# Weight conversion with one VectorE instruction for the low word, two buffers, six weight buffers, and left-over loads by another queue

## The chip, the cores and the metric

The kernel runs on one core of one Trainium2 chip. The metric is the device time of one execution in microseconds (us). One core has five engines with instruction streams of their own: TensorE (matrix products; PE in the profile, its weight loads PEld), VectorE (DVE), ScalarE (ACT), GpSimd (POOL) and SyncE (SP, which here only issues DMA transfers). Each engine works through its stream in the order of the program; semaphores hold an instruction until what it needs is there. ScalarE and GpSimd can issue transfers too.

## The reference

Attention of pooled queries, then a block with a two-dimensional Fourier transform, a normalization and a feed-forward part; cut to what matters:

```python
def _attn_ref(q, k, v):                       # q, k, v: (4, 8, 1152, 64) float32
    q_pool = q.reshape(B, H, S // 2, 2, D).mean(axis=3)
    scores = np.matmul(q_pool, k.transpose(0, 1, 3, 2)) / np.sqrt(D)
    attn = np.exp(scores - scores.max(axis=-1, keepdims=True))
    attn = attn / (attn.sum(axis=-1, keepdims=True) + 1e-9)
    return np.matmul(attn, v)                 # (4, 8, 576, 64)

def _moe_ref(x, w_ch1, w_ch2):                # x: (4, 576, 512); w_ch1 512x2048, w_ch2 2048x512
    u = x + np.real(fft(fft(x, axis=1), axis=2)).astype(np.float32)
    un = (u - mean(u)) / np.sqrt(var(u) + 1e-6)         # over the last axis
    return u + np.maximum(un @ w_ch1, 0.0) @ w_ch2
```

The two weights arrive as float64. There is no such type on the engines, so the kernel takes each number apart by its two 32-bit words.

## The kernel before

**Attention.** There are 32 heads (4 batches of 8), taken two at a time: 16 pairs of 5 units each. For a unit, TensorE makes scores in pieces of 384 columns from a high and a low part of the queries (line 220), VectorE scales each piece into the tile "sp" and keeps a running minimum (line 222), ScalarE takes the exponential (line 234), TensorE transposes the result in groups of four (line 247), ScalarE and sometimes VectorE copy each group out (line 250), and TensorE multiplies with the values (line 263). Ahead of a head, prep_head() has GpSimd add the two halves of each query (line 186) and take the low part of the keys (line 189); the high part of the queries is a cast on ScalarE (line 194), and GpSimd makes the low part "ql" from it (line 197). The loads of a head are issued in lines 126 and 127, the ones for queries, keys and values by SyncE, one by GpSimd.

**After a batch's last head** its middle part runs (dft() and norm(): Fourier products, then a normalization of which lines 550 to 602 concern us), and then its feed-forward part ffn(): 32 blocks in four groups, each group four blocks of the first weight (F1, f1()) and four of the second (F2, f2()). A block is 12 matmuls of 512 columns (lines 689 to 691: three products of high and low parts, four times); after an F1 block ScalarE takes the ReLU (line 708) and VectorE the remainder (line 709). Middle and feed-forward parts of one batch are laid between the attention units of the next by a planner: every step of these generators gives a time in ns, "credit" holds what may still be laid in, and a heap of due times ("after") holds what comes later. The planner's times set the order in which instructions are written, and so the order on each engine. Batches 0 to 2 work on 512 of the 576 columns of a batch; the 64 left over of each are stored to the DRAM tensor "left" (line 608), and the last batch takes these 192 columns as part of its own two blocks of 384 (loaded in lines 593 and 758).

**Conversion.** convert() makes one of the 32 weight blocks usable. It loads 512 KB of words into "wraw" (three buffers), and then: ScalarE the absolute value of the high word ("wa"), VectorE a clamp (631) and a shift and mask (633), ScalarE a scaled copy of the low word into "rest" (635), VectorE the float32 nearest by its bits into "wb" (639) and its power of two back into "wa" (642), ScalarE the high part (646), and GpSimd three passes in two halves each (649): rest times the power of two, the remainder of the high part, their sum. The result goes back to HBM (655) and is loaded again for each use, four times in all, by wload() (681) into one of the three buffers of the pool "w", two blocks ahead. "wa", "rest" and "wb" share the four buffers of the tag "cv". The list "inside" lets one conversion at a time be between its first ScalarE instruction and GpSimd's passes; up to three are under way in all, and a new one begins at the earliest 8 to 10 us of planned time after the last. They are taken in the order in which the feed-forward part wants them: four of W1, four of W2, and so on. I number them 0 to 31.

**The drain.** The tile pool "x" for attention's results has five buffers, so before the attention may go on past a certain point of batch 1, drain() lets the feed-forward part of batch 0 finish, with what conversions are left. Block n of batch 0 waits in the planner until block n + 2's weight is converted.

## Time and profile before

| | us |
|---|---|
| median of 3 runs (lowest to highest) | 1023.06 (1022.12 to 1026.41) |
| time of the profiled execution | 1021.06 |
| its span, first to last instruction | 1019.3 |
| TensorE busy | 968.8 (95%) |
| VectorE busy | 602.5 (59%) |
| ScalarE busy | 529.1 (52%) |
| GpSimd busy | 396.0 (39%) |

The mean granted clock of TensorE is 0.990 of full speed. In forty slices of the span TensorE is at nine tenths or more in most; the other engines are loaded in the first half, where attention and conversions run, and hardly at all in the last eighth, where only the last feed-forward part is left. How to read it: TensorE's busy time is the sum to beat, and what a change elsewhere can win or lose is in TensorE's idle stretches, about 50 us in all, and in stretches at a lower granted clock. A busy share of another engine says little by itself.

### The profile page before, as it was taken

To read this page: it belongs to the slowest core of one execution; us is meant where nothing else is said; L and a number is where in the kernel's file an instruction comes from. 1 tells how busy PE (TensorE), PEld (TensorE's weight loads), DVE (VectorE), ACT (ScalarE), POOL (GpSimd) and SP (SyncE) were. 2 spreads that over 40 slices of the span, in tenths; PEclk is the share of its full clock that TensorE was granted. 3 is DMA by queue.
4 is the path that set the end of the run, shared out by engine and by line. 5 is a ranking of instruction groups with operands and counts; after the bars stand their busy time and mean duration, and the time that the engine had idled before them with its cause. 6 is when DMAs were issued, how large, how long until landed. Compare 5 with 4: busy or idle time off the path is not lost.

```text
span 1019.3 us, 19742 instructions
## 1 busy us (share of the span) xinstructions
PE 968.8 (95%) x7392; PEld 841.5 (83%) x7392; DVE 602.5 (59%) x1526; ACT 529.1 (52%) x1033; POOL 396.0 (39%) x577
## 2 busy tenths in 40 slices
PE   6999988999999999978999999999999999899998
PEld 5898877777788887867888888788888878799998
DVE  5557787888756798866544465745644274422222
ACT  5777877758755575565644454535744221301100
POOL 3555678766666786874523232222400000000000
PEclk9999999999899999999999999999999999999999
DMA  6645458645385877566565453345432445733434
GB/s 181 176 142 183 130 189 255 191 139 167 119 255 208 280 242 235 182 235 197 175 194 164 135 184 120 90 150 161 130 116 83 145 137 165 219 131 128 128 124 124
DMA packets 62515, 170.91 MB, mean 168 GB/s; under 512 B 16770, under 2 KB 20242, under 8 KB 62420
## 3 DMA queue, kind: packets, MB, share of 16 engines
q1 hardware_dynamic: 58100, 151.96, 47.4%
q0 software_dynamic: 4320, 17.70, 5.5%
q8 instruction: 58, 0.95, 0.4%
q14 instruction: 37, 0.30, 0.1%
HBM read 146.88 MB, written 22.75 MB: 166 GB/s over the span
## 4 chain that ended last, share of the span: by engine, by line
PE 51%; DVE 3%; DMA 2%; ACT 1%; issue 1%; POOL 1%; SPq 0%; DVEq 0%; ACTq 0%
PE f L689 7%; PE f L691 6%; PE f L690 6%; PE o L263 6%; PE s L220 6%; PE t L247 5%; PE t L689 5%; PE t L691 5%; PE t L690 5%; DMA w<-w 1%; DVE sp L222 1%; DMA qr<-in_q 1%; PE f L509 1%; PE t L509 1%; ACT pt L250 0%
## 5 line engine op out<-in xcount | busy, mean ns | idle before, releaser
L222 DVE TENSOR_SCALAR_CACHE_REDUCE sp<-s,bia 128x384 f32<-128x384 f32 x288 | 177.5, 616 | 89.6 <-PE s L220 67.5
L220 PE MATMUL s<-ks,qh 128*128 128x384 f32 x480 | 185.1, 386 | 17.3 <-ACT qh L164 6.3
L234 ACT ACTIVATE sp<-sp,bia 128x1152 f32<-128x1152 f32 x144 | 180.2, 1255 | 5.7 <-DVE sp L222 5.4
L250 ACT COPY pt<-t 128x512 f32<-128x512 f32 (+2 forms) x243 | 124.7, 527 | 98.7 <-PE t L247 95.5
L263 PE MATMUL o<-pt,vs 128*64 128x128 f32 (+1 forms) x2880 | 168.1, 271 | 1.1 <-DVE pt L250 0.9
L263 PEld LDWEIGHTS o<-pt,vs 128*64 128x64 f32 x2880 | 148.9, 140 | 23.4 <-issue 20.1
L220 PE MATMUL s<-ks,ql 128*128 128x384 f32 x480 | 164.1, 342 | 0.9 <-POOL ql L197 0.9
L247 PE MATMUL t<-ident,sp 128*128 128x128 f32 x1045 | 151.7, 277 | 3.0 <-DVE sp L222 2.0
L247 PEld LDWEIGHTS t<-ident,sp 128*128 128x128 f32 x1045 | 121.0, 141 | 25.5 <-issue 7.0
L189 POOL TENSOR_TENSOR ks<-kr,ks 64x288 fp32r<-64x288 f32 x120 | 101.9, 880 | 37.3 <-issue 15.9
L220 PEld LDWEIGHTS s<-ks,qh 128*128 128x128 f32 x480 | 92.2, 192 | 28.1 <-ACT pt L250 10.1
L220 PEld LDWEIGHTS s<-ks,ql 128*128 128x128 f32 x480 | 92.6, 193 | 2.1 <-POOL ql L197 1.2
L709 DVE SCALAR_TENSOR_TENSOR g<-f,g 128x512 fp32r<-128x512 f32 (+1 forms) x49 | 32.5, 663 | 99.4 <-ACT g L708 99.4
L708 ACT ACTIVATE g<-f 128x512 fp32r<-128x512 f32 (+1 forms) x49 | 28.2, 576 | 120.0 <-PE f L691 120.0
L222 DVE TENSOR_SCALAR_CACHE_REDUCE sp<-s 128x384 f32<-128x384 f32 x144 | 78.7, 547 | 9.6 <-PE s L220 8.3
L197 POOL TENSOR_TENSOR ql<-qr,qh 128x288 fp32r<-128x288 f32 (+2 forms) x75 | 54.2, 747 | 75.6 <-ACT qh L194 74.6
L689 PE MATMUL f<-unh,w 128*128 128x512 f32 (+1 forms) x196 | 77.4, 395 | 6.3 <-DMA w<-w 5.8
L649 POOL TENSOR_TENSOR rest<-rest,wa 128x256 f32<-128x256 f32 x64 | 48.8, 781 | 88.9 <-DVE wa L642 69.9
L186 POOL TENSOR_TENSOR qr<-qr 128x288 f32<-128x288 f32 x60 | 48.1, 820 | 78.5 <-DMA qr<-in_q 78.5
L689 PE MATMUL f<-g,w 128*128 128x512 f32 (+1 forms) x192 | 76.0, 396 | 2.3 <-DMA w<-w 1.1
L691 PE MATMUL f<-unl,w 128*128 128x512 f32 (+1 forms) x196 | 75.1, 383 | 0.0
L690 PE MATMUL f<-unh,w 128*128 128x512 f32 (+1 forms) x196 | 74.8, 381 | 0.0
(146 smaller groups left out, 1749.8 us busy)
## 6 DMA issues: line engine op xcount, KB each, us to landing
w<-w SPq DMA_DIRECT2D x128, 512.0 KB, 3.6
qr<-in_q SPq DMA_DIRECT2D x30, 576.0 KB, 4.3
ks<-in_k POOLq DMA_DIRECT2D x30, 576.0 KB, 6.2
wraw<-in_w SPq DMA_DIRECT2D x32, 512.0 KB, 3.9
w<-wraw SPq DMA_DIRECT2D x32, 512.0 KB, 3.0
vs<-in_v SPq DMA_DIRECT2D x32, 288.0 KB, 7.0
kr<-in_k SPq DMA_DIRECT2D x30, 288.0 KB, 5.4
out<-x SPq DMA_DIRECT2D x12, 256.0 KB
```

The lines of the kernel that those rows point to most:

```text
L189: nc.gpsimd.tensor_tensor(ks[D:, c], kr[D:, c], ks[D:, c].bitcast(F32), op=ALU.subtract)
L197: nc.gpsimd.tensor_tensor(ql[:, z], qr[:, 0, x:y], qh[:, z].bitcast(F32), op=ALU.subtract)
L220: nc.tensor.matmul(ps, lhsT=l, rhs=k, start=i == 0, stop=i == len(ops) - 1)
L222: nc.vector.tensor_scalar(sp[n, j][:, c], ps, -0.0625, bt[:, pc - 1:pc] if pc else None, op0=ALU.mult, op1=ALU.min, accum_out=bt[:, pc:pc ...
L234: last_exp[0] = nc.scalar.activation(t, t, AF.Exp, bias=bia.pop((n, j))[:, 2:3], scale=-1.0, accum_out=den[pr][:, col:col + 1]).ins
L247: nc.tensor.transpose(ps[:, i * P:i * P + P], sp[k][:, c * P:(c + 1) * P], ident)
L250: (nc.vector.tensor_copy if eng == "v" else nc.scalar.copy)(pt[:, :o], ps[:, :o])
L263: nc.tensor.matmul(po[y * D:y * D + D, :w], lhsT=qkv[2 * pr + y][3][:, c, :], rhs=pt[:, o:o + w], start=c == 0, stop=c == NKC - 1)
L649: nc.gpsimd.tensor_tensor(o[:, c], x[:, c], y[:, c], op=op)
L689: nc.tensor.matmul(ps, lhsT=ah, rhs=bh, start=first, stop=False)
L690: nc.tensor.matmul(ps, lhsT=al, rhs=bh, start=False, stop=False)
L691: nc.tensor.matmul(ps, lhsT=ah, rhs=bl, start=False, stop=last)
```

## The change

Four things change. In convert(), the scaled copy on ScalarE and GpSimd's first pass go; VectorE makes low word times 2^-52 times the power of two in one instruction (line 640 of the new file), written over "wa". So a conversion has two tiles of the tag "cv" instead of three, and GpSimd two passes instead of three. The planner's times in it change: five steps of 700 (or 1000) ns where there were four, 2000 instead of 3000 and 2600 instead of 3000 behind GpSimd's work. When no conversion is left, wload() takes three of six weight tiles from the three "wraw" buffers, so that six are there in all, and ffn() loads up to four blocks ahead. And the loads of the left-over columns in norm() go out by ScalarE's queue instead of SyncE's.

```diff
-                        nc.sync.dma_start(y[i][:, :, HT:].bitcast(F32), left[x, :, 2 * i:2 * i + 2, t * 96:t * 96 + 96])
+                        nc.scalar.dma_start(y[i][:, :, HT:].bitcast(F32), left[x, :, 2 * i:2 * i + 2, t * 96:t * 96 + 96])
@@ convert()
-        yield 6500 if going else 7000
+        yield 7000 if going else 7000
         while inside:
             yield 400
         inside.append(f)
         high, low = w[:, :, 1], w[:, :, 0]
-        a = cvp.tile([P, 512], F32, tag="cv", name="wa", bufs=4)
-        ai = a.bitcast(I32)
+        a, t = (cvp.tile([P, 512], F32, tag="cv", name=x, bufs=4) for x in ("wa", "wb"))
+        ai, ti = a.bitcast(I32), t.bitcast(I32)
+        step = 700 if going else 1000
 
         nc.scalar.activation(a, high.bitcast(F32), AF.Abs)
         yield 900 if going else 1400
         nc.vector.tensor_scalar(a, a, WORD_MIN, WORD_MAX, op0=ALU.max, op1=ALU.min)
-        yield 700 if going else 1000
+        yield step
         nc.vector.tensor_scalar(ai, ai, 3, 0x3FFFFFF8, op0=ALU.logical_shift_left, op1=ALU.bitwise_and)
-        rest = cvp.tile([P, 512], F32, tag="cv", name="rest", bufs=4)
-        nc.scalar.activation(rest, low.bitcast(U32), AF.Copy, scale=2.0 ** -52)
-        yield 700 if going else 1000
-        t = cvp.tile([P, 512], F32, tag="cv", name="wb", bufs=4)
-        b = t.bitcast(I32)
-        nc.vector.scalar_tensor_tensor(b, high, -0x40000000, ai, op0=ALU.bitwise_and, op1=ALU.bitwise_or)
-
-        yield 700 if going else 1000
-        nc.vector.tensor_scalar(ai, b, -0x800000, None, op0=ALU.bitwise_and)
-        yield 700 if going else 1000
+        yield step
+        nc.vector.scalar_tensor_tensor(ti, high, -0x40000000, ai, op0=ALU.bitwise_and, op1=ALU.bitwise_or)
+        yield step
+        nc.vector.tensor_scalar(ai, ti, -0x800000, None, op0=ALU.bitwise_and)
+        yield step
+        nc.vector.scalar_tensor_tensor(a, low.bitcast(U32), 2.0 ** -52, a, op0=ALU.mult, op1=ALU.mult)
+        yield step
         h = w.rearrange("p c x -> p (c x)").rearrange("p (x c) -> p x c", x=2)
         hi, lo = h[:, 0, :], h[:, 1, :]
         nc.scalar.copy(hi.bitcast(F32R), t)
-        for o, x, y, op in ((rest, rest, a, ALU.mult), (t, t, hi.bitcast(F32), ALU.subtract), (lo.bitcast(F32R), t, rest, ALU.add)):
+        for o, x, y, op in ((t, t, hi.bitcast(F32), ALU.subtract), (lo.bitcast(F32R), t, a, ALU.add)):
             for c in (slice(0, 256), slice(256, 512)):
                 nc.gpsimd.tensor_tensor(o[:, c], x[:, c], y[:, c], op=op)
         if not going:
-            yield 3000
+            yield 2000
         inside.pop()
-        yield 3000 if going else 1500
+        yield 2600 if going else 1500
@@ wload()
-        w = wp.tile([P, 2, 512], F32R, tag="w", name=nm)
+        src = (wp, "w", 3)
+        if not todo and not busy:
+            turns[0] += 1
+            if turns[0] % 6 < 3:
+                src = (cvp, "wraw", 3)
+        w = src[0].tile([P, 2, 512], F32R, tag=src[1], name=nm, bufs=src[2])
@@ ffn()
-            load(n + 2)
+            for x in (2,) if todo or busy else (2, 3, 4):
+                load(n + x)
```

The changed planner times move conversions against the rest of the program. GpSimd's stream around conversion 4 (lines 649 before and 647 after; first row the end of conversion 3) and the preparation of the next head of queries (memsets of "qh" and "ql", the sum of q's halves "qr", the low parts "ks" and "ql"), before:

```order
L649 TENSOR_TENSOR wraw<-wb,rest 128x256 x2
L126 DMA ks<-in_k 128x1152
L649 TENSOR_TENSOR rest<-rest,wa 128x256 x2
L649 TENSOR_TENSOR wb<-wb,wraw 128x256 x2
L649 TENSOR_TENSOR wraw<-wb,rest 128x256 x2
L137 MEMSET qh 128x64
L138 MEMSET ql 128x64
L186 TENSOR_TENSOR qr<-qr 128x288 x2
L189 TENSOR_TENSOR ks<-kr,ks 64x288 x4
L197 TENSOR_TENSOR ql<-qr,qh 128x288 x2
```

And after:

```order
L647 TENSOR_TENSOR wraw<-wb,wa 128x256 x2
L126 DMA ks<-in_k 128x1152
L137 MEMSET qh 128x64
L138 MEMSET ql 128x64
L186 TENSOR_TENSOR qr<-qr 128x288 x2
L189 TENSOR_TENSOR ks<-kr,ks 64x288 x4
L197 TENSOR_TENSOR ql<-qr,qh 128x288 x2
L647 TENSOR_TENSOR wb<-wb,wraw 128x256 x2
L647 TENSOR_TENSOR wraw<-wb,wa 128x256 x2
```

The conversion that stood ahead of the head's preparation stands behind all of it.

GpSimd's stream at the last head ahead of the drain, whose "ql" rows are the last of line 197 before the drain; the numbers tell tiles apart. Before:

```order
L649 TENSOR_TENSOR wb_5636<-wb_5636,wraw_5428 128x256 x2
L649 TENSOR_TENSOR wraw_5428<-wb_5636,rest_5617 128x256 x2
L137 MEMSET qh_5734 128x64
L138 MEMSET ql_5735 128x64
L186 TENSOR_TENSOR qr_5571<-qr_5571 128x288 x2
L189 TENSOR_TENSOR ks_5570<-kr_5572,ks_5570 64x288 x4
L197 TENSOR_TENSOR ql_5735<-qr_5571,qh_5734 128x288
L197 TENSOR_TENSOR ql_5735<-qr_5571,qh_5734 128x224
L197 TENSOR_TENSOR ql_5735<-qr_5571,qh_5734 128x64
L649 TENSOR_TENSOR rest_5726<-rest_5726,wa_5675 128x256 x2
L649 TENSOR_TENSOR wb_5758<-wb_5758,wraw_5588 128x256 x2
```

And after:

```order
L186 TENSOR_TENSOR qr_5432<-qr_5432 128x288 x2
L189 TENSOR_TENSOR ks_5431<-kr_5433,ks_5431 64x288 x4
L647 TENSOR_TENSOR wb_5475<-wb_5475,wraw_5342 128x256 x2
L647 TENSOR_TENSOR wraw_5342<-wb_5475,wa_5474 128x256 x2
L197 TENSOR_TENSOR ql_5587<-qr_5432,qh_5586 128x288
L197 TENSOR_TENSOR ql_5587<-qr_5432,qh_5586 128x224
L197 TENSOR_TENSOR ql_5587<-qr_5432,qh_5586 128x64
L647 TENSOR_TENSOR wb_5616<-wb_5616,wraw_5511 128x256 x2
L647 TENSOR_TENSOR wraw_5511<-wb_5616,wa_5615 128x256 x2
L647 TENSOR_TENSOR wb_5685<-wb_5685,wraw_5636 128x256 x2
```

Before, conversion 26 is the last ahead of the head's preparation and 27 is the first behind "ql"; after, the one between "ks" and "ql" is 24, and 25 and 26 follow. So 27 conversions stood ahead of that "ql", and 25 stand there now. TensorE has eight feed-forward blocks of batch 0 in the drain before, nine after; up to about 375 us of the trace its stream is the same in both.

SyncE's stream at the start of batch 3 (weights "w", results "out", the left-over columns "unh" and "unl"), before:

```order
L681 DMA w_10208<-w_15_6019 128x1024
L723 DMA out<-x 128x512
L593 DMA unh_10227<-left 128x2x96
L593 DMA unh_10228<-left 128x2x96
L593 DMA unl_10229<-left 128x2x96
L593 DMA unl_10230<-left 128x2x96
L593 DMA unh_10243<-left 128x2x96
L593 DMA unh_10244<-left 128x2x96
L593 DMA unl_10245<-left 128x2x96
L593 DMA unl_10246<-left 128x2x96
L681 DMA w_10257<-w_0_1465 128x1024
L723 DMA out<-x 128x512
```

And after:

```order
L684 DMA w_10073<-w_15_5923 128x1024
L684 DMA w_10099<-w_0_1463 128x1024
L727 DMA out<-x 128x512
L684 DMA w_10148<-w_1_1689 128x1024
L727 DMA out<-x 128x512
L684 DMA w_10165<-w_2_1903 128x1024
```

The eight transfers from "left" are gone from here, and the first weight of batch 3 (source w_0) directly follows the last of batch 2. On ScalarE they stand in two groups of four, each ahead of two of the four casts of line 599 that batch 3 needs (before, the casts follow line 571 at once):

```order
L571 ACTIVATE dg<-ident,vt 96x96 x6
L593 DMA unh_10118<-left 128x2x96
L593 DMA unh_10119<-left 128x2x96
L593 DMA unl_10120<-left 128x2x96
L593 DMA unl_10121<-left 128x2x96
L599 CAST unh_10118<-d 128x2x288
L599 CAST unh_10119<-d 128x2x288
L593 DMA unh_10134<-left 128x2x96
L593 DMA unh_10135<-left 128x2x96
L593 DMA unl_10136<-left 128x2x96
L593 DMA unl_10137<-left 128x2x96
L599 CAST unh_10134<-d 128x2x288
```

The order on TensorE has three feed-forward blocks of batch 2 behind line 581's two matmuls and ahead of batch 3's first block, where two stood before.

## Rows read from the trace of the kernel before

**Rows 1.** Stretches: bounds, length, busy PE, PEld, DVE, ACT, POOL; clock, DMA share, GB/s.

```profile
87.00:275.00 188.00, 171.68 (x1581) 145.27 (x1579) 150.31 (x388) 142.12 (x282) 131.27 (x187) 0.96 0.56 175
...
430.00:478.00 48.00, 38.70 (x225) 31.39 (x225) 31.57 (x57) 27.21 (x48) 33.67 (x47) 0.93 0.67 226
```

**Rows 2.** TensorE's waits, 87 to 275 us: total us, times, longest us.

```profile
PE f L247 <- ACT pt L250: 3.7, 5, 1.6
PE s L220 <- ACT pt L250: 3.2, 5, 1.1
PE s L220 <- DVE sp L222: 2.3, 4, 0.8
...
PE t L247 <- DVE sp L222: 1.2, 2, 0.7
```

**Rows 3.** TensorE's waits for weight loads: whole run, then 430 to 478 us.

```profile
PE f L689 <- DMA w<-w: 6.8, 3, 3.1
...
PE f L689 <- DMA w<-w: 4.1, 2, 3.1
```

**Rows 4.** Groups by line, 87 to 275 us: busy us, mean ns, idle ahead.

```profile
L635 ACT ACTIVATE rest<-wraw 128x512 f32<-128x512 uint32 x13 | 9.0, 689 | 0.0
...
L649 POOL TENSOR_TENSOR rest<-rest,wa 128x256 f32<-128x256 f32 x25 | 18.5, 756 | 41.7 <-DVE wa L642 38.4 <-ACT wraw L646 3.3
...
L639 DVE SCALAR_TENSOR_TENSOR wb<-wraw,wa 128x512 int32<-128x512 int32 x13 | 12.5, 963 | 0.1
```

**Rows 5.** Three lines of the conversion, whole run: ns least/middle/most, first to last us.

```profile
L639 DVE SCALAR_TENSOR_TENSOR wb<-wraw,wa x32: 670/690/3799, 93.6 to 470.6; 128x512 int32<-128x512 int32 x32
...
L642 DVE TENSOR_SCALAR wa<-wb x32: 408/422/1047, 95.3 to 471.3; 128x512 int32<-128x512 int32 x32
...
L646 ACT CAST wraw<-wb x32: 605/622/627, 95.6 to 471.3; 128x512 fp32r<-128x512 f32 x32
```

**Rows 6.** Timeline near 158 us: start us, length us, engine; idle time ahead in brackets.

```profile
157.12 0.67 ACT L194 CAST qh<-qr 128x576 fp32r<-128x576 f32 x1 [3.37 <-POOL qr L186]
...
158.33 0.45 PE L220 MATMUL s<-ks,qh 128*128 128x384 f32 x1 [1.14 <-ACT pt L250]
...
159.93 3.85 PE L263 MATMUL o<-pt,vs 128*64 128x128 f32 x36
```

**Rows 7.** Stretch 160 to 163.5 us, columns as in rows 1.

```profile
160.00:163.50 3.50, 3.50 (x35) 3.50 (x36) 1.62 (x6) 3.13 (x6) 3.00 (x4) 0.51 0.58 98
```

**Rows 8.** Timeline of the drain; SPq is SyncE's queue of transfers.

```profile
445.57 1.59 POOL L649 TENSOR_TENSOR wraw<-wb,rest 128x256 fp32r<-128x256 f32 x2
...
447.19 0.32 SPq L655 DMA_DIRECT2D w<-wraw  x1
...
450.86 0.43 SPq L620 DMA_DIRECT2D wraw<-in_w  x1
...
454.22 0.77 PE L689 MATMUL f<-unh,w 128*128 128x512 f32 x1 [3.09 <-DMA w<-w]
...
467.71 0.39 PE L689 MATMUL f<-g,w 128*128 128x512 f32 x1
...
470.55 2.19 PE L263 MATMUL o<-pt,vs 128*64 128x128 f32 x36
...
477.41 0.33 SPq L655 DMA_DIRECT2D w<-wraw  x1
```

**Rows 9.** Timeline behind the drain: a load of queries, and a wait.

```profile
483.06 0.42 SPq L126 DMA_DIRECT2D qr<-in_q  x1
...
493.51 0.45 PE L220 MATMUL s<-ks,qh 128*128 128x384 f32 x1 [1.77 <-ACT pt L250]
```

**Rows 10.** Timeline at the start of batch 3.

```profile
873.34 0.98 SPq L593 DMA_DIRECT2D unh<-left  x2
...
877.70 0.41 SPq L681 DMA_DIRECT2D w<-w  x1
...
881.38 0.41 PE L689 MATMUL f<-unh,w 128*128 128x384 f32 x1 [2.69 <-DMA w<-w]
```

1 line of the change is left out of this document (added).

## The prediction, made before the result was known

> **What bounds the kernel now.** I read the stretches first. TensorE works nearly all the time, so a change pays only where TensorE waits or runs on its lower clock level. It waits in three places that this change touches. Between 87 and 275 us it is busy 171.7 of 188 us at a mean granted clock of 0.96, with VectorE at 150.3 us (80%), ScalarE at 142.1 and GpSimd at 131.3 [rows 1]: here attention, the first Fourier stage and weight conversions share three engines. Between 430 and 478 us it is busy 38.7 of 48 us at clock 0.93 [rows 1]: the drain of batch 0, where feed-forward blocks follow each other and each needs a weight that has only just been converted. And it stands once near 880 us, at the start of batch 3. In between it has hardly any gaps.
>
> The waits say who ends them. From 87 to 275 us the four largest entries are 3.7 and 3.2 us ended by ScalarE's copies of transposes and 2.3 and 1.2 us ended by VectorE's score pieces [rows 2]. Waits of TensorE for a weight load come to 6.8 us in the whole run, three of them, and two with 4.1 us are in the drain [rows 3]; the third, 6.8 - 4.1 = 2.7 us, is the one near 880 us.
>
> **One conversion.** Removed: ScalarE's scaled copy of the low word, 13 in the stretch 87 to 275 for 9.0 us, and GpSimd's product in two halves, 18.5 us there [rows 4]. Added: one VectorE instruction with two inputs from SBUF, of the shape and kind of line 639. That line takes 0.67 us at the least, 0.69 in the middle, 3.80 at worst [rows 5], and 0.963 on average in this stretch [rows 4]. I take 0.69: 13 x 0.69 = 9.0 us more on VectorE, 150.3 + 9.0 = 159.3 of 188 us (85%). So VectorE does not become the bound on average, but it works in program order, and a score piece behind the new instruction comes 0.69 us later. Which part lands on the path? Of the 10.4 us in the four entries, VectorE ended 3.5 (34%) [rows 2]; 0.34 x 9.0 = 3.1 us. The bounds are 0 (hidden in VectorE's idle 20%) and 9.0 (all on the path).
>
> Against it stands the relief. At 157 us ScalarE sat 3.37 us on the cast of q, because GpSimd added q's halves only after a conversion; the transposes' copies stood behind that cast, TensorE waited 1.14 us for one of them, and soon after, its next 36 matmuls took 3.85 us [rows 6]. From 160 to 163.5 us the granted clock was 0.51, which is the lower of the engine's two levels, 1.2 GHz [rows 7]; a group of the same shape at the higher one takes 2.19 [rows 8]. In the new order GpSimd has that conversion behind q's halves, not before them. I count the 1.14 and the 3.85 - 2.19 = 1.7, that is 2.8 us. Of the other ScalarE-ended waits, 6.9 - 1.1 = 5.8 us, I take a third, 1.9, since GpSimd loses one of three equal parts of each conversion. Together 4.7; the bounds are 0 (a new wait forms elsewhere) and 8.6 (all of them go). Net of this stretch: 3.1 - 4.7 = **-1.6 us**.
>
> The Trainium skill, page "SBUF — State Buffer", section "Who interferes with whom", says that a VectorE instruction with two SBUF inputs contends with a GpSimd instruction that reads SBUF, and the second to issue blocks until the first is done. Line 639's middle value of 0.69 us, next to its least, shows that most are not blocked [rows 5]. By the page alone every overlap would cost up to one GpSimd operation; the second rival below prices that from rows.
>
> **Two buffers, and where the conversions stand.** Before, three tiles of the four-deep tag "cv" go into a conversion, so its third tile waits for GpSimd's last addition of the conversion before; now two go in, and conversion n needs only n-2 finished. That allows overlap. But the planner's steps changed too: a conversion holds "inside" for five steps instead of four. The order shows the effect: before the drain GpSimd has 27 conversions (0 to 26) ahead of the last remainder of q; now 25. Two more conversions therefore fall into the drain, and one more feed-forward block (nine instead of eight).
>
> The drain's price, by rows. Before: GpSimd ends conversion 27 at 445.57 + 1.59 = 447.16 us, SyncE writes it out at 447.19, and TensorE starts on it, loaded back, at 454.22 after a wait of 3.09 [rows 8]: 7.1 us from GpSimd's end to TensorE. Four writes later it is 477.41, so 7.6 us apiece. The last block, on weight 29, ends where the next attention group starts, 470.55 [rows 8].
>
> After: conversion 25 stands where 27 stood. Its own GpSimd part is 1.5 us shorter, and I give it 1 us more because one block fewer is ahead: written at 447.2 - 2.5 = 444.7. What sets the pace from there? Three raw buffers, and VectorE works off a block's remainder between two steps of a later conversion, so three conversions form a ring: write to TensorE 7.0, block 470.55 - 467.71 = 2.8 [rows 8], ReLU and remainder 1.3 (two passes of that size, 0.62 + 0.69), mask 0.42, new product 0.69, high part 0.62 [rows 5], GpSimd 4 x 0.76 = 3.0 [rows 4]: 15.8 us, or 5.3 per conversion. Weight 29 is written at 444.7 + 4 x 5.3 = 465.9, TensorE starts on it at 473.0 and ends at 475.8, against 470.55: **+5.3 us**. Bounds: if SyncE's pair is the limit (447.19 to 450.86 + 0.43 is 4.1 us [rows 8]) the end is 444.7 + 16.4 + 7.1 + 2.8 = 471.0, +0.5. At the pace of before, 7.6, it is 485.0, +14.4. The lower clock level in the longer waits is inside that upper bound. I take 5.3: the wait of one conversion for the one before, which the pace of 7.6 holds, is gone, and the ring is what is left.
>
> After the drain a wait goes: at 493.51 TensorE waits 1.77 us on a chain that begins at q's load, issued at 483.06 behind a weight's write [rows 9]. With attention about 5 us later and that load not later, the wait is covered: **-1.8** (0 if the load slips as well).
>
> **Left-over columns by ScalarE's queue, six weight buffers.** SyncE issues eight transfers from "left" ahead of batch 3's first weight, 0.98 us for two of them; the weight goes out at 877.70 and TensorE waits 2.69 us until 881.38 [rows 10]. Four pairs at 0.98 are 3.9 us, so without them the weight lands before it is wanted: **-2.7**. On ScalarE's queue they cost the same 3.9 us, two groups of 1.9, each ahead of two casts that batch 3's first block needs, and the VectorE remainders wait for those. The cover is TensorE's: the order has three feed-forward blocks (3 x 2.8 = 8.4 us) behind line 581's matmuls and ahead of batch 3's first block, where two stood. Two groups of issue and four casts fit. If they do not, up to 1.9 us comes back. Loads four blocks ahead instead of two gain nothing else: only three weight waits exist [rows 3], and two lie in the drain, where the new depth is not yet on. Their price is none that I see: the "wraw" tiles that lend room hold no conversion any more by then.
>
> **Sum.** -1.6 + 5.3 - 1.8 - 2.7 = -0.8 us. The profiled execution took 1021.06 us (span 1019.3), 2.0 under the median 1023.06; on the median's base **1022.3 us**. About 0.5% (5.1 us) is what a measurement of this kernel can tell from no change.
>
> **Rivals.** First, the drain costs nothing: conversions overlap so well in their two buffers that SyncE's 4.1 us is the pace (+0.5), and the early relief is full (8.6 against 3.1): -5.5 + 0.5 - 1.8 - 2.7 = -9.5, **1013.6 us**. For it: the conversions' engines are at 57 to 70% in the drain [rows 1], and the wait for the predecessor is the one that two buffers remove. Against it: VectorE's and ScalarE's program order ties each conversion to a block two or three back.
>
> Second, slower: VectorE is blocked beside GpSimd from 87 to 275 us. The new instruction then costs 0.963 us like line 639 there [rows 4], 12.5 us in all, and as ScalarE's score work waits on VectorE, half of it lands on the path without any relief: +6.3 + 5.3 - 1.8 - 2.7 = +7.1, **1030.2 us**. It decides against the kernel once over 4.3 of the 12.5 us land there (4.3 + 5.3 - 4.5 = 5.1). This is what the rule of the Trainium skill told above would give if it held at every overlap. Against it: the middle one of the 32 instructions of line 639 takes 0.69, near their least of 0.67 [rows 5], and GpSimd has a third less to do.
>
> Third, the drain keeps its pace of 7.6: -1.6 + 14.4 - 4.5 = +8.3, **1031.4 us**. For it: two more conversions stand there. Against it: two buffers.
>
> Fourth, the last part does not do what it says: ScalarE's queue delays batch 3's casts as long as SyncE delayed the weight. Then the 2.7 stays: **1025.0 us**.
>
> **How the numbers follow.** Forecast 0.36; first rival 0.33, its milder forms (1013 to 1018) with it; second 0.14; third 0.10; fourth 0.07. The forecast's own range is 1018 to 1028, the drain at +1 at one end and at +11, short of the pace of before, at the other; 0.01 of it I count past each bound. Faster is 0.33 + 0.01 = 0.34, same 0.34 + 0.07 = 0.41, slower 0.14 + 0.10 + 0.01 = 0.25. The whole range reaches down to 1012, 1.6 under the first rival's full form, and up to 1032, just past the third.
>
> **What would show it.** Right: VectorE some 9 us busier and ScalarE 9 and GpSimd 18 us less busy from 87 to 275; in the drain TensorE waiting for weight loads several times, with SyncE's writes 5 us apart and the next attention group starting near 475; no wait for a weight at batch 3's start. Wrong: writes 4 us apart, or an attention group after the drain that starts before 470; VectorE's new instruction near 1 us; or a lower granted clock in stretches that had none.

## The result: 0.8% slower

The changed kernel takes 1029.48 us (median of 7 runs, 1025.22 to 1032.13) against 1022.12 us of the kernel before beside it (7 runs). The ratio is 1.0079, with a 95% interval of 1.0051 to 1.0107. Forecast were 1022.3 us and no change that a measurement can tell; the time lies inside the range of 1012 to 1032, on the side that had a chance of 0.25.

The profiled execution of the changed kernel has a span of 1030.3 us, 11.0 more than before. The stretches that answer to [rows 1], with the same columns:

```profile
87.00:275.00 188.00, 173.04 (x1648) 147.23 (x1647) 160.77 (x417) 138.25 (x276) 120.85 (x168) 0.99 0.57 181
...
430.00:478.00 48.00, 32.39 (x107) 23.96 (x106) 32.42 (x56) 18.83 (x35) 23.75 (x30) 0.79 0.55 189
```

From 87 to 275 us TensorE gets more done than before (1648 matmuls instead of 1581). Its granted clock is 0.99 instead of 0.96, but that is not shown to come from the change: e4_six below, whose program is that of before up to here, has 0.99 too, and e3_left, of which the same holds, has 0.95. VectorE is 10.5 us busier, GpSimd 10.4 and ScalarE 3.9 less; that is for more attention in the same time. From 430 to 478 us it is the other way round: 107 matmuls instead of 225, and a clock of 0.79 instead of 0.93. Of the 225, 97 stand behind the drain, which ended at 470.55 us before and goes on past 478 now.

TensorE's waits, in all (total us, times, longest): for weights in the whole run, which answers [rows 3]; and the three largest from 87 to 275 us, which answer [rows 2].

```profile
PE f L693 <- DMA w<-w: 12.1, 4, 4.2
...
PE o L263 <- DVE pt L250: 3.0, 3, 1.6
PE s L220 <- DVE sp L222: 2.9, 5, 0.8
PE f L247 <- ACT pt L250: 2.8, 3, 2.2
```

All four waits for a weight are in the drain now; the one near 880 us is gone. In the early part the two entries of ScalarE's copies are 2.8 and 1.1 us where they were 3.7 and 3.2, and VectorE's share has grown, as the prediction had it.

The new VectorE instruction in the whole run (ns least/middle/most), and from 87 to 275 us (busy us, mean ns):

```profile
L640 DVE SCALAR_TENSOR_TENSOR wa<-wraw,wa x32: 670/687/1289, 96.2 to 482.5; 128x512 f32<-128x512 uint32 x32
...
L640 DVE SCALAR_TENSOR_TENSOR wa<-wraw,wa 128x512 f32<-128x512 uint32 x12 | 9.5, 792 | 0.0
```

Its middle value of 0.687 us is the 0.69 that was taken from line 639 [rows 5]; the mean of 0.79 in the early part is between that and the 0.963 of the second rival. The mean comes from few instructions. Five of the 32 took 0.75 us or more, four of them in this stretch, and at each of the five a GpSimd instruction was under way when it began, as here:

```profile
188.38 1.08 POOL L186 TENSOR_TENSOR qr<-qr 128x288 f32<-128x288 f32 x1 [8.48 <-DMA qr<-in_q]
188.72 1.29 DVE L640 SCALAR_TENSOR_TENSOR wa<-wraw,wa 128x512 f32<-128x512 uint32 x1
```

At 188.72 us GpSimd had 0.74 us left, and VectorE took 0.60 longer than 0.69. In the other four GpSimd had 0.20 to 0.48 us left, and the excess is again 0.13 to 0.14 us less than that. Of the remaining 27, which took 0.67 to 0.69 us, one began with GpSimd under way, with 0.13 us left. So the trace agrees with the rule of the Trainium skill (page "SBUF — State Buffer", section "Who interferes with whom") wherever VectorE came second; that was seldom so. The middle value, which the prediction held against the second rival, says no more than that.

To see where the 11 us arise, take fixed marks in TensorE's stream: the starts of the attention groups of line 263, of which there are 80. In the 38th group both kernels have done 7 feed-forward blocks, in the 48th (the first behind the drain) 30, so these marks compare like with like. Times in us from the span's start:

| kernel | 13th | 38th | 48th | 52nd | span |
|---|---|---|---|---|---|
| before | 98.65 | 314.10 | 470.55 | 495.86 | 1019.3 |
| changed | 97.97 | 306.87 | 485.73 | 508.99 | 1030.3 |

Up to the 13th group the two differ by 0.7, and do so from the first group on, ahead of any conversion. From the 13th to the 38th the changed kernel gains 6.6 us; from there to the 48th it loses 178.86 - 156.45 = 22.4; from the 48th to the 52nd it gains 25.31 - 23.26 = 2.1; behind that, 523.4 - 521.4 = 2.1 more (of the spans to two places). At the 48th group the changed kernel is 485.73 - 470.55 = 15.2 us late. So the question is twofold: where do 6.6 us of gain come from, and 22.4 of loss?

### The profile page after: what moved, and what is told of

Its sections match the earlier page's. It is cut to its first block, busy times and chain, and to the rows that moved or that the text cites. A ratio compares the mean times of both kernels' runs of the same rounds, so it can differ in the third digit from the quotient of the medians.

```text
span 1030.3 us, 19692 instructions
## 1 busy us (share of the span) xinstructions
PE 971.8 (94%) x7392; PEld 841.6 (82%) x7392; DVE 619.1 (60%) x1558; ACT 512.5 (50%) x1001; POOL 354.8 (34%) x513
## 4 chain that ended last, share of the span: by engine, by line
PE 50%; DMA 2%; DVE 2%; ACT 1%; issue 1%; SPq 0%; DVEq 0%; ACTq 0%
PE f L693 6%; PE o L263 6%; PE s L220 6%; PE f L695 6%; PE f L694 6%; PE t L247 5%; PE t L693 5%; PE t L695 5%; PE t L694 5%; DMA wraw<-in_w 1%; PE f L509 1%; DVE sp L222 1%; DMA w<-wraw 1%; DMA w<-w 0%; ACT pt L250 0%
## 5 line engine op out<-in xcount | busy, mean ns | idle before, releaser
L263 PE MATMUL o<-pt,vs 128*64 128x128 f32 (+1 forms) x2880 | 165.1, 267 | 4.8 <-DVE pt L250 4.6
L263 PEld LDWEIGHTS o<-pt,vs 128*64 128x64 f32 x2880 | 145.8, 138 | 27.4 <-issue 20.2
L220 PEld LDWEIGHTS s<-ks,qh 128*128 128x128 f32 x480 | 91.6, 191 | 25.1 <-DVE sp L222 10.2
L713 DVE SCALAR_TENSOR_TENSOR g<-f,g 128x512 fp32r<-128x512 f32 (+1 forms) x49 | 32.5, 664 | 101.9 <-ACT g L712 101.9
L647 POOL TENSOR_TENSOR wb<-wb,wraw 128x256 f32<-128x256 f32 x64 | 47.4, 761 | 130.2 <-ACT wraw L644 110.3
L712 ACT ACTIVATE g<-f 128x512 fp32r<-128x512 f32 (+1 forms) x49 | 28.3, 577 | 123.8 <-PE f L695 123.8
L693 PE MATMUL f<-unh,w 128*128 128x512 f32 (+1 forms) x196 | 79.2, 404 | 10.3 <-DMA w<-w 9.8
L197 POOL TENSOR_TENSOR ql<-qr,qh 128x288 fp32r<-128x288 f32 (+2 forms) x75 | 57.5, 791 | 79.0 <-ACT qh L194 78.2
L694 PE MATMUL f<-unh,w 128*128 128x512 f32 (+1 forms) x196 | 76.5, 390 | 0.0
L186 POOL TENSOR_TENSOR qr<-qr 128x288 f32<-128x288 f32 x60 | 50.2, 855 | 71.6 <-DMA qr<-in_q 71.5
```

The source lines that it names most:

```text
L186: nc.gpsimd.tensor_tensor(qr[:, 0, c], qr[:, 0, c], qr[:, 1, c], op=ALU.add)
L197: nc.gpsimd.tensor_tensor(ql[:, z], qr[:, 0, x:y], qh[:, z].bitcast(F32), op=ALU.subtract)
L220: nc.tensor.matmul(ps, lhsT=l, rhs=k, start=i == 0, stop=i == len(ops) - 1)
L263: nc.tensor.matmul(po[y * D:y * D + D, :w], lhsT=qkv[2 * pr + y][3][:, c, :], rhs=pt[:, o:o + w], start=c == 0, stop=c == NKC - 1)
L693: nc.tensor.matmul(ps, lhsT=ah, rhs=bh, start=first, stop=False)
L694: nc.tensor.matmul(ps, lhsT=al, rhs=bh, start=False, stop=False)
```

## Experiments

The first theory (A): the planner's fifth step holds the row of conversions up, so fewer are done when the drain begins, and the drain pays. Its rival (B): the new VectorE instruction, standing between a block's remainder and GpSimd, lengthens the drain itself. All kernels were timed beside the kernel before. The expectations count conversions by the order of the instructions (27 ahead of the drain before, 24 in the changed kernel); in the traces 25 and 23 have been written to HBM by the start of the 47th group, the last ahead of the drain.

### The arithmetic alone, with the old planner times (e1_arith)

```diff
-        rest = cvp.tile([P, 512], F32, tag="cv", name="rest", bufs=4)
-        nc.scalar.activation(rest, low.bitcast(U32), AF.Copy, scale=2.0 ** -52)
...
         nc.vector.tensor_scalar(ai, b, -0x800000, None, op0=ALU.bitwise_and)
+        nc.vector.scalar_tensor_tensor(a, low.bitcast(U32), 2.0 ** -52, a, op0=ALU.mult, op1=ALU.mult)
         yield 700 if going else 1000
...
-        for o, x, y, op in ((rest, rest, a, ALU.mult), (t, t, hi.bitcast(F32), ALU.subtract), (lo.bitcast(F32R), t, rest, ALU.add)):
+        for o, x, y, op in ((t, t, hi.bitcast(F32), ALU.subtract), (lo.bitcast(F32R), t, a, ALU.add)):
```

> The kernel before with the new arithmetic alone (VectorE's product, two tiles, two GpSimd passes), the product written in the planner step of the mask, so that all planner times are those of before; 27 conversions stand ahead of the drain as before. Theory A: the changed kernel lost its time since the planner's fifth step slows the row of conversions and leaves two more to the drain. Then the attention group that follows the drain starts here at 470 us or earlier (after: 485.7), the early part is 2 to 7 us shorter, and the whole is at 1014 to 1020 us. Rival B: the new VectorE instruction itself, standing between a block's remainder and GpSimd, slows the drain. Then that group starts at 480 us or later, and the whole is at 1026 us or more.

Measured: 1020.1 us, ratio 0.9984 (0.9966 to 1.0001). The 48th group starts at 470.17, as before, so rival B falls in its plain form. But the 2 to 7 us less in the early part did not come either: the 38th group starts at 314.88. The early gain is not from cheaper conversions. The stretch shows a trade:

```profile
87.00:275.00 188.00, 167.54 (x1588) 141.32 (x1585) 157.82 (x400) 134.79 (x267) 114.65 (x162) 1.00 0.57 176
```

The clock is at 1.00 throughout (before: 0.96), yet TensorE is busy 4.1 us less than before, for as many matmuls (1588 and 1581). From the 13th group to the 38th the trace of before has 15.8 us between TensorE's matmuls and 13.7 us at the lower clock level; with the new arithmetic it is 20.2 and none. What the clock gave back, waits took. But this trade is not shown to come from the arithmetic, since it is there without it. The same stretch of e4_six, which runs the program of before up to here:

```profile
87.00:275.00 188.00, 168.26 (x1584) 142.04 (x1583) 148.16 (x388) 143.09 (x283) 130.81 (x186) 0.99 0.56 175
```

From the 13th group to the 38th e4_six has 19.6 us between the matmuls and 3.4 at the lower level, and takes 215.6 us; before it was 215.4.

### The planner times alone, with the old arithmetic (e2_steps)

```diff
-        yield 6500 if going else 7000
+        yield 7000
...
         nc.vector.tensor_scalar(ai, b, -0x800000, None, op0=ALU.bitwise_and)
         yield 700 if going else 1000
+        yield 700 if going else 1000
...
-            yield 3000
+            yield 2000
         inside.pop()
-        yield 3000 if going else 1500
+        yield 2600 if going else 1500
```

> The kernel before with the new planner times alone: five steps instead of four (one empty), and the new waits; the arithmetic, the three tiles and GpSimd's three passes are those of before. Theory A: the drain grows as it did in the changed kernel, the group that follows it starts at 480 to 492 us, and the whole is at 1030 to 1042 us. Rival B: the drain is as before within 3 us, and the whole at 1019 to 1025 us. A side question is where the changed kernel's 7 us up to 340 us came from: if from cheaper conversions, they are missing here; if from conversions further apart, they are here too.

Measured: 1029.74 us, ratio 1.0087 (1.0066 to 1.0107): a loss as large as that of the changed kernel, without one instruction changed. The 38th group starts at 306.86 (changed kernel: 306.87), so the early gain is from the steps too. TensorE's waits for weights, and the 48th group:

```profile
PE f L690 <- DMA w<-w: 10.2, 4, 3.2
...
480.86 1.31 PE L263 MATMUL o<-pt,vs 128*64 128x128 f32 x20
```

480.86 is 10.3 us after the kernel before and 4.9 ahead of the changed one. So the steps make two thirds of the loss at this mark; the last 4.9 us come only when new steps and new arithmetic meet. They stand at the last weight that the drain waits for, 29. Its write and its load by SyncE, in e2_steps:

```profile
469.78 0.32 SPq L656 DMA_DIRECT2D w<-wraw  x1
472.92 0.32 SPq L682 DMA_DIRECT2D w<-w  x1
```

In the changed kernel these are at 471.28 and 477.63 (the chain is shown further down): 1.5 us of the 4.9 are the later write, and 3.2 are the time from it to the load, 6.35 instead of 3.14. In e2_steps the weight load and the raw load ahead of this write went out 2.9 and 2.5 us before it, in the changed kernel 1.0 and 0.6.

How the steps lose it is read from SyncE's writes of conversions 14 and 23 (line 655 before, line 653 in the changed kernel), the stretch in which batch 0's feed-forward blocks are already laid between attention units. Before, and then changed:

```profile
305.99 0.33 SPq L655 DMA_DIRECT2D w<-wraw  x1
398.08 0.32 SPq L655 DMA_DIRECT2D w<-wraw  x1
```

```profile
311.95 0.32 SPq L653 DMA_DIRECT2D w<-wraw  x1
420.46 0.33 SPq L653 DMA_DIRECT2D w<-wraw  x1
```

Nine conversions take 92.1 us before, 10.2 each, and 108.5 changed, 12.1 each. With the arithmetic alone they take 10.2 each, with the steps alone 11.9. Conversion 25 is written at 420.4 before and at 444.6 changed, 24 us later. Ahead of batch 0's feed-forward part the planned times of a conversion add up to the same in both kernels (1000 ns more in the steps, 1000 less behind GpSimd's work), and write 13 goes out at 297.0 and 298.0 us; from there on a conversion is planned 800 ns longer. So the pace is lost only there; what the steps change in the early part is where a conversion's instructions stand, GpSimd's one step later. The drain ends when weight 29 is ready, however early TensorE came to it.

### Left-over loads alone, and six buffers alone (e3_left, e4_six)

```diff
-                        nc.sync.dma_start(y[i][:, :, HT:].bitcast(F32), left[x, :, 2 * i:2 * i + 2, t * 96:t * 96 + 96])
+                        nc.scalar.dma_start(y[i][:, :, HT:].bitcast(F32), left[x, :, 2 * i:2 * i + 2, t * 96:t * 96 + 96])
```

> The kernel before with the eight loads from left on ScalarE's queue, nothing else. If SyncE's issue time delayed the first weight of batch 3, the wait of 2.7 us near 880 us is gone, and the whole is 2 to 3 us less, 1019 to 1020 us. If the loads cost ScalarE what they cost SyncE, the wait of 2.7 us has another place near 880 us, and the whole is the same.

The second has the new wload() and the loads up to four ahead, and the left-over loads still on SyncE:

```diff
-            load(n + 2)
+            for x in (2,) if todo or busy else (2, 3, 4):
+                load(n + x)
```

> The kernel before with six weight buffers and loads up to four blocks ahead once no conversion is left, nothing else. If depth alone is enough, the first weight of batch 3 goes out ahead of the eight loads from left, and the wait of 2.7 us near 880 us is gone here too: 1019 to 1020 us. If it is not, the wait stays, and the whole is the same, 1022 us. Neither theory on the drain expects a change there.

Measured: 1018.48 us, ratio 0.9978 (0.9958 to 0.9997), and 1016.44 us, 0.9947 (0.9925 to 0.9970). With the queue alone a wait of 1.29 us stays, until 883.27 us; with the depth alone TensorE is busy 8.00 of 8 us from 878 to 886. From the 80th group to the end it is 224.2 us before, 222.8 with the queue and 221.2 with the depth. Each does part of the same thing, and the depth is enough. The measured 0.53% for the depth is more than those 2.9 us (0.29%), though its interval reaches to 0.30%.

The two also show something on the wait of [rows 9]. From the 51st to the 52nd group the kernel before takes 8.4 us, e3_left 6.35 and e4_six 10.6, with the same program up to there. The 2.1 us that the changed kernel gained at this place (6.35 again) are a difference between executions, not an effect.

### All of the change with the old planner times (e5_all_old_steps)

The edit is that of e1_arith together with those of e3_left and e4_six.

> The changed kernel with the planner times of before (the product in the step of the mask, the old waits); the left-over loads on ScalarE's queue and six buffers as changed. 27 conversions are written ahead of the drain, as before (changed kernel: 24). Theory A, the number of conversions that are done when the drain begins decides: the group after the drain starts at 469 to 472 us as with the new arithmetic alone, the wait near 880 us is gone, and the whole is at 1014 to 1018 us. Rival C, the six buffers or the loads on ScalarE's queue work against the drain: that group starts at 476 us or later, the whole at 1022 us or more.

Measured: 1016.02 us, ratio 0.9954 (0.9936 to 0.9972); 48th group at 469.63. As theory A has it: with the old times the change is a gain of half a per cent. Of the 5.8 us by which the spans differ, 2.9 lie behind the 80th group and 2.1 at the wait of [rows 9], which comes and goes between executions.

### The start of the conversions (e6_early, e7_before_late, e8_best, e12_early20)

Each moves the first conversion by one number: the changed kernel to 35000 (e6) and to 20000 (e12), the kernel before to 83000 (e7), the kernel of e5 to 30000 (e8).

```diff
-    cdue = 60000.0
+    cdue = 35000.0
```

> The changed kernel as it is, with the first conversion 25 us of planned time earlier (35000 instead of 60000); 27 conversions are written ahead of the drain, as before, with the new steps. Theory A: the group after the drain starts at 468 to 476 us, the whole is at 1012 to 1021 us; the 7 us gained up to 340 us shrink by what three more conversions cost there, 2 to 3 us each. Rival D, the slower pace of the steps holds up the drain itself: that group starts at 480 us or later and the whole stays at 1026 us or more.

> The kernel before with the first conversion 23 us of planned time later (83000 instead of 60000), nothing else: 25 conversions are written ahead of the drain instead of 27. Theory A, with the prices that the run of the steps alone gave for three conversions (7.2 us less early, 17.5 us more in the drain): 5 us less up to 340 us, 12 us more in the drain, the whole at 1026 to 1030 us. Rival D: neither changes by more than 3 us, the whole at 1020 to 1025 us.

> The changed kernel with the planner times of before and the first conversion 30 us of planned time earlier (30000): 29 conversions are written ahead of the drain. Theory A, at 2.4 us early and 5.8 us in the drain for each: 5 us more up to 340 us, 8 to 12 us less in the drain, 3 to 7 us below the same kernel that starts at 60000, so 1008 to 1014 us. If a conversion ahead of 87 us costs more than one after it (the first attention groups), or the drain is then bound by TensorE, the two are the same.

> The changed kernel with the first conversion at 20000 instead of 60000, its own steps; 29 conversions are written ahead of the drain. Theory A by number: the group after the drain at 458 to 466 us, the whole at 1003 to 1012 us. Against it, by place: conversions among the first three pairs hold up attention groups, and the early part is 5 us or more above that of the start at 35000 (302.2 us at the start of the 38th group).

| kernel | time us | ratio (95%) | 38th | 48th | span |
|---|---|---|---|---|---|
| e6_early | 1022.75 | 1.0021 (0.9999 to 1.0042) | 302.24 | 470.43 | 1020.0 |
| e7_before_late | 1039.91 | 1.0188 (1.0161 to 1.0214) | 308.56 | 482.26 | 1037.1 |
| e8_best | 1029.92 | 1.0092 (1.0068 to 1.0117) | 327.54 | 486.05 | 1029.2 |
| e12_early20 | 1024.44 | 1.0018 (0.9998 to 1.0038) | 316.69 | 479.05 | 1022.8 |

e7 gains 5.5 us up to the 38th group, as expected, and loses 17.2 from there to the 48th, more than the 12 expected, with the old arithmetic and the old steps: conversions that come later are enough to lose the drain. From the 48th to the 52nd it takes 29.3 us (before 25.3), and ends above the expected 1026 to 1030 us. e6 gets the drain back, though only to 470.43 from an early part that was 11.9 us ahead, and its time is above the expected 1012 to 1021: its row still has the pace of the new steps, 12.3 us each from write 14 to write 23. In e8 and e12 the expectations by number fail: 13.4 and 2.6 us more up to the 38th group. The price of a conversion in the early part is not a constant; that expectation was wrong.

### Another queue for the writes (e9_pool_write)

```diff
-        nc.sync.dma_start(d, h.bitcast(F32))
+        nc.gpsimd.dma_start(d, h.bitcast(F32))
```

> The changed kernel; only the write of a converted weight goes out by GpSimd's queue instead of SyncE's. In the drain of the changed kernel a write that follows a weight load and a raw load within 1.3 us takes 6.0 to 6.4 us until the next load of that weight can go out, and 2.7 us otherwise. Theory E, the write stands behind 1 MB of loads in one queue: from write to load 4 us or less in every case, the group after the drain starts at 478 to 483 us (485.7), the whole is at 1023 to 1027 us. Rival F, the engines of the transfers are simply full, whatever the queue: 6 us stay, and the group starts at 484 us or later.

Measured: 1032.41 us, ratio 1.0090 (1.0058 to 1.0122); 48th group at 485.52. Three writes on GpSimd, each with the load of the same weight on SyncE behind it:

```profile
454.46 0.57 POOL L653 DMA_DIRECT2D w<-wraw  x1 [0.30 <-POOL wraw L647]
459.04 0.32 SPq L684 DMA_DIRECT2D w<-w  x1
459.93 0.57 POOL L653 DMA_DIRECT2D w<-wraw  x1 [0.30 <-POOL wraw L647]
466.15 0.32 SPq L684 DMA_DIRECT2D w<-w  x1
466.19 0.57 POOL L653 DMA_DIRECT2D w<-wraw  x1 [0.30 <-POOL wraw L647]
472.59 0.32 SPq L684 DMA_DIRECT2D w<-w  x1
```

4.6, 6.2 and 6.4 us: the long ones stay, so theory E falls. Which queue a write is in does not decide; that a weight load and a raw load of 512 KB each are under way with it may. In the changed kernel the engines of the transfers have busy shares of 0.78 to 1.06 in each us from 457 to 462, between the write at 456.62 and its load at 462.99, and 0.08 in the next, as rival F has it.

### The fifth step left out where it costs (e10_merged, e11_merged_early, f3_merged45, f4_merged28)

```diff
-        yield 7000 if going else 7000
+        yield 6500 if going else 7000
...
         nc.vector.tensor_scalar(ai, ti, -0x800000, None, op0=ALU.bitwise_and)
-        yield step
+        if not going:
+            yield step
```

That is e10, against the changed kernel; e11, f3 and f4 start the first conversion at 35000, 45000 and 28000 besides.

> The changed kernel with the planner's fifth step left out only from the start of batch 0's feed-forward part on (the product in the step of the mask there, and the old wait of 6500); ahead of that the slower steps stay. 26 conversions are written ahead of the drain (24 in the changed kernel, 27 before). Theory A: 7 us less up to 340 us as in the changed kernel, since the row of conversions there is the same; the drain ends when its weights are ready, so the group after it starts at 473 to 479 us, and the whole is at 1017 to 1022 us. Rival D, the drain's own chain sets its end: 483 us or later, 1026 us or more.

> The kernel of the run above with the first conversion at 35000 instead of 60000; 28 conversions are written ahead of the drain. Theory A: 10 to 12 us less up to 340 us, as with the early start alone, and the group after the drain at 460 to 467 us; the whole is at 1004 to 1012 us. If the number that is ready matters less than where each conversion falls among the attention groups, the early part comes out another way, as with the start at 30000 and the old steps (13 us more).

> The fastest kernel so far (the changed kernel, the product in the step of the mask from batch 0's feed-forward part on, first conversion at 35000) with the first conversion at 45000; 28 conversions are written ahead of the drain in both. If the number written decides and the slower steps of the early part are what helps there: 1005 to 1013 us again, the 38th group's start at 302 to 308 us. If 35000 was a lucky place among the attention groups, 1015 us or more.

> As the run above, with the first conversion at 28000; 29 are written ahead of the drain. By number: 1002 to 1010 us. By place: a start at 20000 and one at 30000 (with the old steps) had put conversions among the first pairs of attention, with 5 to 13 us more up to the 38th group; then 1012 us or more.

| kernel | time us | ratio (95%) | 38th | 48th | span |
|---|---|---|---|---|---|
| e10_merged | 1018.62 | 0.9965 (0.9939 to 0.9990) | 306.97 | 471.55 | 1015.2 |
| e11_merged_early | 1007.95 | 0.9843 (0.9812 to 0.9874) | 303.74 | 459.73 | 1003.0 |
| f3_merged45 | 1009.28 | 0.9872 (0.9845 to 0.9900) | 311.36 | 464.69 | 1008.3 |
| f4_merged28 | 1011.41 | 0.9891 (0.9861 to 0.9922) | 311.83 | 465.79 | 1009.8 |

e10 shows theory A most plainly: one step less and the old wait of 6500, and only from batch 0's feed-forward part on, bring the row from write 14 to write 23 to 10.7 us each, take 14.2 us off the 48th group and leave the early gain as it was. It also shows that this early gain is worth nothing by itself: e1 and e10 reach the 38th group at 314.88 and 306.97, and the 48th at 470.17 and 471.55. The rest of the conversions end the drain in both.

e11, f3 and f4 bring the conversions forward as well, and are faster than the kernel before by 1.1 to 1.6%, and so than the changed one. At the 38th group e11 and f4 have both written 17 weights, and are 8 us apart: the early part goes by where conversions fall among the attention groups. (f3's 38th group is outside the expected 302 to 308 us, and f4's time lies between its two ranges.) The drain goes by when its last weights are done: in 16 of the 18 traces the 48th group starts 9.2 to 14.4 us after weight 29 is written. The number that is written ahead does not fix that alone: by the 47th group e11 and e12 have both written 27, but weight 29 at 447.47 and 464.96 us. In e8 and f4, the other two traces, it is 30.6 and 22.8 us; there weight 29 came too early to decide. e11's stretch from the 47th group to the 48th, for ten blocks, is 45.4 us; before it is 50.5.

### Two in the drain, and two tiles (f1_ring2, f2_cv2)

f1_ring2 allows two conversions under way instead of three from the start of the drain on ("draining" is filled there and stays so):

```diff
-        if now >= cdue and todo and len(busy) < 3:
+        if now >= cdue and todo and len(busy) < (2 if draining else 3):
```

> The changed kernel; in the drain at most two conversions are under way instead of three (their raw loads begin later), nothing else. Theory G, the drain's pace is a ring of three conversions, 23.2 us around in the changed kernel (write, load, block, remainder, the next product, high part, GpSimd, write), 6.7 to 7.7 each: with two the ring gives 9 to 11.6 each, the group after the drain starts at 494 to 505 us, the whole is at 1038 to 1049 us. Rival H, one engine or the transfers set the pace, not the ring: 6.7 to 7.5 each as before, the group starts at 484 to 488 us.

f2_cv2 takes the second buffer away:

```diff
-        a, t = (cvp.tile([P, 512], F32, tag="cv", name=x, bufs=4) for x in ("wa", "wb"))
+        a, t = (cvp.tile([P, 512], F32, tag="cv", name=x, bufs=2) for x in ("wa", "wb"))
```

> The changed kernel with two tiles of the tag cv instead of four, so that a conversion begins only when GpSimd has ended the one before it, as the three tiles of before nearly forced. If the overlap by two buffers is worth what the prediction took it for (2.3 us for each conversion in the drain, 7.6 to 5.3), the group after the drain starts 6 us or more later than 485.7, and the whole is 1035 us or more. If the ring sets the pace and one conversion's start is not in it, both are as in the changed kernel within 3 us.

f1_ring2: 1034.15 us, ratio 1.0116 (1.0082 to 1.0151), but the 48th group starts at 483.61, 2.1 us earlier than in the changed kernel. What it loses comes behind the drain: 29.0 us to the 52nd group instead of 23.3. SyncE's queue in its drain (L685 loads a weight, L620 the next raw words):

```profile
452.17 0.32 SPq L653 DMA_DIRECT2D w<-wraw  x1
455.35 0.32 SPq L685 DMA_DIRECT2D w<-w  x1
455.72 0.42 SPq L620 DMA_DIRECT2D wraw<-in_w  x1
459.60 0.32 SPq L653 DMA_DIRECT2D w<-wraw  x1
462.29 0.32 SPq L685 DMA_DIRECT2D w<-w  x1
462.65 0.43 SPq L620 DMA_DIRECT2D wraw<-in_w  x1
467.25 0.32 SPq L653 DMA_DIRECT2D w<-wraw  x1
```

Two conversions take 15.1 us, 7.5 each; theory G wanted 9 to 11.6 and falls. With two under way the ring is shorter: a weight's load goes out 2.7 to 3.2 us after its write, not 6.0 to 6.4.

f2_cv2: 1051.71 us, ratio 1.0288 (1.0253 to 1.0324). With two tiles in all the changed kernel is 22 us slower. It loses most of that ahead of the drain: 38th group at 315.56, 47th at 432.21 (414.15 in the changed kernel), 48th at 506.97. In the drain writes are 7.6 us apart instead of 6.7, a difference of 0.9 and not 2.3. This does not price the step from the kernel before, whose three of four tiles are a looser rule than two of two: e2_steps has that arrangement and writes 25 to 29 at 6.6 us apart, e7_before_late at 6.8. Against it the second buffer gains nothing in the drain.

## Why the prediction was wrong

**The forecast.** It had the drain at +5.3 us and everything else as small gains. The step that failed is the drain's term: at the 48th group the changed kernel is 15.2 us late. Its pace of 5.3 us for each conversion was measured at 6.7, and the 9.9 us from weight 29's write to the end at 14.4. The loss in the drain and the gain ahead of it both come from the planner's times. For the drain the prediction had reduced them to one sentence, "Two more conversions therefore fall into the drain". Its sum has a second fault: the 5.3 is the difference of two absolute times, the end of the last block at 475.8 against 470.55, worked out from when weights are written. A gain ahead of the drain does not move that end and cannot be added to it, so the -1.6 had no place there. e1 and e10 show it: 8 us apart at the 38th group, 1.4 at the 48th.

**The drain's term.** The mechanism was right in its order, and the start was right: conversion 25 was to be written at 444.7 us, and was at 444.58. That was in part luck, for the 1.5 us taken off for a shorter GpSimd part are not what made it: e2_steps, with GpSimd's three passes, writes it at 443.51. Two sizes were off, the pace and the end. Its ring from write to write of the same buffer was put at 15.8 us, and is 20 to 23. The chain of the changed kernel's drain, from the write of weight 27 to the write of conversion 30, and the last block:

```profile
456.62 0.32 SPq L653 DMA_DIRECT2D w<-wraw  x1
...
462.99 0.32 SPq L684 DMA_DIRECT2D w<-w  x1
463.35 0.43 SPq L620 DMA_DIRECT2D wraw<-in_w  x1
...
466.82 0.48 PE L693 MATMUL f<-unh,w 128*128 128x512 f32 x1 [2.69 <-DMA w<-w]
...
469.02 0.68 ACT L630 ACTIVATE wa<-wraw 128x512 f32<-128x512 f32 x1 [1.78 <-DMA wraw<-in_w]
...
471.28 0.32 SPq L653 DMA_DIRECT2D w<-wraw  x1
471.45 0.60 ACT L712 ACTIVATE g<-f 128x512 fp32r<-128x512 f32 x1 [1.75 <-PE f L695]
472.08 0.69 DVE L713 SCALAR_TENSOR_TENSOR g<-f,g 128x512 fp32r<-128x512 f32 x1 [0.48 <-ACT g L712]
473.35 0.42 DVE L638 TENSOR_SCALAR wa<-wb 128x512 int32<-128x512 int32 x1
474.35 0.69 DVE L640 SCALAR_TENSOR_TENSOR wa<-wraw,wa 128x512 f32<-128x512 uint32 x1
...
475.11 0.62 ACT L644 CAST wraw<-wb 128x512 fp32r<-128x512 f32 x1
475.81 1.85 POOL L647 TENSOR_TENSOR wb<-wb,wraw 128x256 f32<-128x256 f32 x2 [5.68 <-ACT wraw L644]
...
477.63 0.32 SPq L684 DMA_DIRECT2D w<-w  x1
...
479.86 0.32 SPq L653 DMA_DIRECT2D w<-wraw  x1
...
481.36 0.76 PE L693 MATMUL f<-g,w 128*128 128x512 f32 x1 [2.29 <-DMA w<-w]
...
485.73 2.19 PE L263 MATMUL o<-pt,vs 128*64 128x128 f32 x36
```

The prediction's order is there: weight to TensorE, ReLU (L712), remainder (L713), then conversion 30's mask and product (L638, L640), its high part and GpSimd. But from write to TensorE it is 466.82 - 456.62 = 10.2 us and not 7.0, since the write takes 6.4 until the load can go out; a block takes 4.4 to 4.6 and not 2.8, for much of it runs at the lower clock level; and from ReLU to write it is 8.4 where 6.0 were counted, as two products of the norm stand in VectorE's order too (line 596, at 472.68 and 473.68 us). So weight 29 is written at 471.28, (471.28 - 444.58) / 4 = 6.7 apiece and not 5.3, and from there to the end it is 14.4 us (6.3 to the load, 3.7 to TensorE, 4.4 for the block) and not 9.9. 26.7 + 14.4 = 41.1 against 31.1 makes the 10 us between +5.3 and +15.2. f1_ring2 shows that the ring is not a fixed length, so that it was a poor way to work out a pace. What sets 6.6 to 7.6 us in all these kernels stays open: neither the arithmetic (e2_steps has 6.6), nor the writes' queue (e9_pool_write has 6.6), nor the number under way alone. The order in which a conversion's instructions stand between the drain's blocks was not varied by itself.

**The early part.** The net of -1.6 mixes two causes. Its cost of 3.1 and 1.9 of its relief come from the arithmetic, +1.2 together; the arithmetic alone takes 215.1 us from the 13th group to the 38th, where before it was 215.4: -0.3, within what executions of one program differ by (217.4 in e3_left, the program of before up to there). The other 2.8 of the relief come from the new order of GpSimd's work, which is the planner's, and here the steps alone give 6.8. So this term had the right sign and was too small. It was read from one wait of ScalarE for q's halves, 3.37 us at 157 us; from 87 to 275 us there are five such waits, 9.5 us in all, and 3.6 with the steps alone. That they are the cause is not shown: the arithmetic alone brings them to 2.5 us and gains nothing. The bounds held. The four entries called the largest of [rows 2] also leave out one of 1.3 us, which the profile puts down to no engine.

**Behind the drain.** -1.8 was forecast and 2.1 seen, but e3_left shows the same without the cause that was named. One wait in one profiled execution was taken for a property of the kernel; that the number fitted was luck.

**Batch 3.** -2.7 was forecast; from the 80th group on, with one block (2.8 us) more to do than before, the changed kernel takes 224.3 us against 224.2. The size of that term was right, its cause only in part: the queue, which was to give all of it, gives 1.4 us alone, and the depth, which was put at nothing, gives 2.9 alone. The fourth rival falls.

**The rivals.** The first, with the drain at +0.5, falls with the drain's term. The second had the mechanism of the new instruction's longer times, but these come to 1.4 us in all 32 instructions, and the drain's loss is there without them (e2_steps). Its 0.963 rests mostly on one instruction of 3.80 us [rows 5]. The third, the drain at its pace of before, put the end of the drain at 485.0 us, and it was 485.73; it took 7.6 us apiece where 6.7 were measured, and 9.9 us behind the last write where it was 14.4, so that its two errors nearly cancel. It had a chance of 0.10. The reason "Against it: two buffers" did not hold, since kernels with three of four tiles reach 6.6 to 6.8 as well (e2_steps, e7_before_late).

## What to carry to other kernels

A step that a planner adds to a chain of which few may be under way can slow the whole row, even when no engine has more to do (10.2 to 11.9 us each in e2_steps): compare the pace of such a row, from the trace or by its place in the order of instructions, at several points before pricing the instructions themselves. Where a stretch ends with the slowest of two rows, time won in the other one is waited away; the row of conversions ends the drain here, and bringing it forward (e11_merged_early) gained 1.6%. A wait, or a lower clock, that stands once in one profile should be looked for in a second execution of the same program before its removal is counted.

## What the runs showed of the hardware

The granted clock follows TensorE's waits in the drain. From the 47th group to the 48th, before and then changed:

```profile
420.01:470.55 50.54, 41.23 (x209) 33.05 (x208) 35.81 (x67) 26.51 (x49) 35.42 (x47) 0.93 0.66 233
```

```profile
414.15:485.73 71.58, 52.83 (x224) 40.48 (x223) 50.22 (x91) 28.03 (x49) 36.21 (x48) 0.83 0.61 206
```

Before, 6.8 us of it are at 0.5; in the changed kernel, with 18.8 us of idle time there instead of 9.3, it is 23.9 us. A block of twelve matmuls then takes 4.4 to 4.6 us instead of 2.8, so a late weight is paid for twice.

A write of 512 KB lets the load behind it go out after 2.7 us when it is alone. It takes 3.1 to 3.5 us when a weight load and a raw load went out 2.5 to 3.2 us ahead of it (e2_steps), and 6.0 to 6.4 us when they went out within 1.3 us ahead of it (the changed kernel); on another queue it is no better (6.2 and 6.4). One of 4.4 us, with the loads 3.6 to 3.9 us ahead, shows that the distance is not all.

A VectorE instruction with two inputs from SBUF that began while a GpSimd instruction was under way took longer by what GpSimd had left, less 0.13 to 0.14 us, in all five cases of line 640 in the changed kernel.
